# Attention with a gated feed-forward on one core: K turned as five windows of row pairs, x rows four to a partition, and a reordered opening of head 0 with norms on GpSimd

## The chip, the cores and the metric

The kernel runs on one core of one Trainium2 chip. The time is the device time of one execution in microseconds, and less is better. Executions are repeated in rounds, each round running the kernel in question and the kernel before on the same chip. The profile is one traced execution. Its engines are PE (TensorE, matmuls), PEld (its weight loads), DVE (VectorE), ACT (ScalarE), POOL (GpSimd) and SP (the engine that issues most DMAs). A program on one core has no second die to compare with.

## The reference, cut to what matters

```python
x:  (1, 2048, 640) bf16      k_cache, v_cache: (1, 32, 2048, 192) bf16
wq: (640, 32*192)            wo: (32*192, 640)       w1, w3: (640, 1536)   w2: (1536, 640)

xn = layernorm(x)                                   # over the 640 columns
q  = (xn @ wq) as 32 heads of 192
p  = softmax(q k^T * 192**-0.5)                     # 2048 x 2048 for each head
s  = concat_heads(p v) @ wo
g  = silu((silu(xn @ w1) * (xn @ w3)) @ w2)
out = x + s * g
```

## The kernel before

The 32 heads run one after the other as a stream of steps. A head has four blocks `qb` of 512 queries, a block has eight steps `p` of 256 keys. A step is: six score matmuls into a PSUM tile `st2`, one exponential of 128x1024 on ACT, and 16 value matmuls. Scores are written two steps ahead of values. At the start of block `qb` of head `h` stands the projection of q for head `h + 1`, block `qb`, so q is always one head ahead. Head 0 is special: nothing stands ahead of it, so x must be loaded, normed and transposed, K of head 0 must be transposed on PE, and q of head 0 itself must be projected block by block. This opening and head 0 are what the change rewrites.

K is needed transposed. It has 192 columns a key, and its matmuls go in pairs, one on rows 0 to 63 of PE and one on rows 64 to 127, which overlap (in the trace of the kernel before the two of a score pair start 18 ns apart and last 376 ns each). So the kernel before keeps three tiles a head: two from the transposing DMA, and KC, which two further DMAs fill with halves moved to the other 64 rows.

```python
def load_k(h):                                     # heads 1 to 31
    kh = A_k_cache[0, h]
    KA = kvp.tile([P, SK], BF16, ...); nc.sync.dma_start_transpose(out=KA[:], in_=kh[:, 0:P])
    KB = kvp.tile([P, SK], BF16, ...); nc.sync.dma_start_transpose(out=KB[:], in_=kh[:, DH - P:DH])

def copy_k(h):                                     # for h == 0 the same by ACT and DVE
    nc.gpsimd.dma_start(out=KC[64:P, :], in_=KA[0:64, HK:SK])
    nc.gpsimd.dma_start(out=KC[0:64, :], in_=KB[64:P, 0:HK])

def emit_scores(h, qb, p):                         # cut: each row is a pair, rows 0-63 and rows 64-127 of PE
    rounds = [(KA[0:64, lo], qAB[0][0:64, :], KA[64:P, hi], qAB[0][64:P, :]),
              (KB[0:64, lo], qC[0:64, 0, :],  KB[64:P, hi], qAB[1][64:P, :]),
              (KC[0:64, lo], qC[0:64, 1, :],  KC[64:P, lo], qC[64:P, 0, :])]

def ln_norm(g, i2):                                # cut; x group g of 512 rows is four tiles of 128
    for k in range(2):
        nc.vector.tensor_scalar(out=xn[:], in0=x_sb[:, 4 * g + i, :], scalar1=mv[:, i, 0:1], scalar2=rstd[:, i, 0:1],
                                op0=ALU.subtract, op1=ALU.mult)
        for c in range(DC):
            nc.tensor.transpose(out=pst[:, k, c, :], in_=xn[:, c * P:(c + 1) * P], identity=ident_bf[:])
    # cut: one copy to xnT, and after i2 == 1 two DMAs to xnS, the copy of xnT with its halves exchanged

# the opening, cut
transpose_k0(); ln_norm(0, 0); ln_norm(0, 1); project0(0, 1); project0(0, 0); copy_k(0)
for i in range(4): ln_stats(1, i)                  # DVE statistics; the power 1/sqrt runs on GpSimd
scores(0)
load_w(1); load_k(1); load_v(1)                    # W, K, V of head 1; load_w issues from GpSimd
scores(1)

for n, (h, qb, p) in enumerate(stream):            # cut
    if p == 0 and n > 0: project(h + 1, qb)
    scores(n + 2)
    if h == 0 and qb == 0 and p == 5: project(1, 0)          # the first use of W of head 1
    values(n)
    if h == 0 and qb + 1 < NQB:
        if p == 1 or p == 2: ln_norm(qb + 1, p - 1)
        if p == 3: project0(qb + 1, 1); project0(qb + 1, 0)  # q of head 0, next block
```

## Time and profile before

| | kernel before |
|---|---|
| time, median of 3 runs | 1957.51 us (1957.27 to 1957.65) |
| span of the profiled run | 1955.9 us |
| first exponential of head 0 (timeline) | 25.23 us |
| first exponential of head 1 (timeline) | 91.80 us |
| from head to head after that | 50.69 us |
| after the last exponential | 293.0 us |

The two lines that say what bounds it, from the page of the kernel before: the busy time of each engine with its share of the span, and the shares of the chain of work that ended last.

```profile
PE 1937.5 (99%) x27351; PEld 1390.2 (71%) x27351; DVE 654.1 (33%) x989; ACT 1184.2 (61%) x1277; POOL 319.2 (16%) x572
...
PE 98%; DVE 1%; DMA 1%; ACT 0%; issue 0%; DVEq 0%; ACTq 0%
```

PE is the bound nearly everywhere. What is left is in the table of waits of PE (kernel before; columns: who waited for what, total us, times, longest us):

```profile
engine line waited for: us in total, times, longest us
PE pk L255 <- DMA vt<-in_A_k_cache_dram: 4.6, 1, 4.6
PE warm L501 <- POOL ident_bf masks.py:199: 2.8, 1, 2.8
PE obank L449 <- DVE osum L459: 1.6, 2, 0.8
...
```

In the timeline of the kernel before (start, duration, engine, line, instruction), GpSimd issues the three loads of W of head 1 at 30.17 us, and the first projection that reads them starts at 38.47 us, after they have landed (35.28 us for the last):

```profile
30.17 0.89 POOL L225 DMA_DIRECT2D W<-in_A_wq_dram  x1
...
31.77 0.72 POOL L230 DMA_DIRECT2D W<-in_A_wq_dram  x1
...
38.47 0.37 PE L360 MATMUL ps<-xnT,W 64*128 64x512 bf16 x1
```

### The profile page before, as it was taken

The page shows a single profiled execution, that of the slowest core. Times are in us where ns is not written, and L with a number is a line of the kernel's source. Part 1 is how long each engine was busy: PE and PEld are TensorE (multiplying, and loading weights), DVE is VectorE, ACT ScalarE, POOL GpSimd, SP SyncE. Part 2 cuts the span into 40 slices and gives each one's busy share as a digit, 9 for nine tenths or more (in the row PEclk, how much of TensorE's full clock was granted, in tenths as well). Part 3 has the DMA queues.
Part 4 walks back from the last instruction along what each step waited for, and adds up shares of the span by engine and source line. Part 5 has one row for each costly group of instructions (what it writes and reads, how often), then busy time and mean ns, then how long its engine had stood idle before and what let it go on. Part 6 is the DMA issues. An engine that isn't in the chain of part 4 may idle for free.

```text
span 1955.9 us, 59887 instructions
## 1 busy us (share of the span) xinstructions
PE 1937.5 (99%) x27351; PEld 1390.2 (71%) x27351; DVE 654.1 (33%) x989; ACT 1184.2 (61%) x1277; POOL 319.2 (16%) x572
## 2 busy tenths in 40 slices
PE   7999999999999999999999999999999999999998
PEld 5677777777777777777777777777777777577776
DVE  5433333333333333333333333333333334521111
ACT  4667676767776767777777767776767777210000
POOL 3211111111111111111111111111111110000000
PEclk9999999999999999999999999999999999999999
DMA  7323232424343433363433243433323230937772
GB/s 178 80 65 93 59 96 67 94 64 100 68 100 68 100 68 97 67 160 68 100 68 100 65 99 68 97 71 77 88 57 93 58 85 2 247 69 140 155 152 60
DMA packets 362020, 177.95 MB, mean 91 GB/s; under 512 B 305712, under 2 KB 348976, under 8 KB 361760
## 3 DMA queue, kind: packets, MB, share of 16 engines
q1 hardware_dynamic: 334512, 116.21, 27.5%
q0 software_dynamic: 22736, 54.43, 11.3%
q8 instruction: 216, 3.54, 0.8%
q10 hardware_dynamic: 4512, 3.41, 0.6%
q14 instruction: 44, 0.36, 0.1%
HBM read 52.82 MB, written 27.79 MB: 41 GB/s over the span
## 4 chain that ended last, share of the span: by engine, by line
PE 98%; DVE 1%; DMA 1%; ACT 0%; issue 0%; DVEq 0%; ACTq 0%
PE obank L449 35%; PE st L420 31%; PE ps L360 14%; PE ps_s L106 11%; PE st L421 3%; PE ps_f L615 3%; PE ps_gu L589 1%; DMA vt<-in_A_k_cache_dram 1%; PE ps L341 0%; ACT pT L423 0%; DVE stats L295 0%; PE pst L311 0%; PE pk L255 0%; DMA qC<-qA 0%; ACT xnT L314 0%
## 5 line engine op out<-in xcount | busy, mean ns | idle before, releaser
L423 ACT ACTIVATE pT<-st 128x1024 bf16<-128x1024 f32 x1024 | 1046.3, 1022 | 257.5 <-PE st L421 242.0
L449 PEld LDWEIGHTS <-pT 64*128 64x128 bf16 x16384 | 743.2, 94 | 212.7 <-issue 2.5
L449 PE MATMUL obank<-vt,pT 64*128 64x193 bf16 x16384 | 866.2, 243 | 1.6 <-DVE osum L459 1.6
L420 PE MATMUL st<-qA,KA 64*128 64x512 bf16 x1024 | 385.4, 376 | 1.6 <-ACT pT L423 0.9
L420 PE MATMUL st<-qC,KB 64*128 64x512 bf16 x1024 | 385.3, 376 | 0.7 <-DMA qC<-qA 0.5
L420 PE MATMUL st<-qC,KC 64*128 64x512 bf16 x1024 | 385.3, 376 | 0.8 <-DVE KC L264 0.8
L421 PE MATMUL st<-qA,KA 64*128 64x512 bf16 x1024 | 385.6, 377 | 0.0
L421 PE MATMUL st<-qB,KB 64*128 64x512 bf16 x1024 | 385.5, 376 | 0.0
L421 PE MATMUL st<-qC,KC 64*128 64x512 bf16 x1024 | 385.5, 376 | 0.0
L458 DVE COPY osum<-obank 128x772 f32<-128x772 f32 x128 | 123.2, 962 | 784.0 <-PE obank L449 784.0
L360 PE MATMUL ps<-xnT,W 64*128 64x512 bf16 x1280 | 299.3, 376 | 0.0
L360 PE MATMUL ps<-xnS,W 64*128 64x512 bf16 x1280 | 294.0, 377 | 0.0
L330 POOL DMA_DIRECT2D qC<-qA x127 | 67.1, 528 | 1239.4 <-DVE rl_all L465 1235.9
L360 PEld LDWEIGHTS <-W 64*128 64x128 bf16 x2560 | 141.9, 94 | 104.8 <-issue 0.2
L366 ACT CAST qB<-ps 128x512 bf16<-128x512 f32 x128 | 74.9, 585 | 222.0 <-PE ps L360 222.0
L106 PE MATMUL ps_s<-wo_sb,oT 128*128 128x256 bf16 (+3 forms) x1536 | 208.8, 300 | 0.0
L106 PEld LDWEIGHTS <-oT 128*128 128x128 bf16 x1536 | 148.1, 98 | 60.7
L420 PEld LDWEIGHTS <-KC 64*128 64x128 bf16 x1024 | 96.4, 94 | 106.1 <-DVE KC L264 1.1
L459 DVE TENSOR_TENSOR osum<-osum,obank 128x772 f32<-128x772 f32 x128 | 122.7, 958 | 13.3
L466 DVE TENSOR_TENSOR ostage<-osum,rl_all 128x768 bf16<-128x768 f32 x128 | 122.6, 958 | 4.4
L401 DVE SCALAR_TENSOR_TENSOR hT<-pt,qB 64x512 bf16<-64x512 bf16 x64 | 43.8, 684 | 204.2 <-ACT pt L400 204.2
L420 PEld LDWEIGHTS <-KA 64*128 64x128 bf16 x1024 | 96.4, 94 | 15.8 <-issue 1.3
(77 smaller groups left out, 1151.1 us busy)
## 6 DMA issues: line engine op xcount, KB each, us to landing
vt<-in_A_v_cache_dram SPq DMA_DIRECT2D x32, 768.0 KB, 6.1
o_scr<-ostage SPq DMA_DIRECT2D x16, 1536.0 KB, 9.3
qC<-qA POOLq DMA_DIRECT2D x254, 64.0 KB, 1.9
qC<-qB POOLq DMA_DIRECT2D x127, 64.0 KB, 2.3
wo_sb<-in_A_wo_dram POOLq DMA_DIRECT2D x1, 7680.0 KB, 35.2
W<-in_A_wq_dram POOLq DMA_DIRECT2D x32, 160.0 KB, 3.3
KC<-KA POOLq DMA_DIRECT2D x31, 128.0 KB, 5.5
KC<-KB POOLq DMA_DIRECT2D x31, 128.0 KB, 5.5
```

Of the source, the lines that this page charges most:

```text
L106: nc.tensor.matmul(ps[:, 0:w], lhsT=oT[:, k, :], rhs=wo_sb[:, k, c0:c1], start=(k == 0), stop=(k == OC - 1))
L330: nc.gpsimd.dma_start(out=qC[0:64, half, :], in_=qAB[half][64:P, :])
L360: nc.tensor.matmul(ps[:, r * 512:(r + 1) * 512], lhsT=W[rows, j, :], rhs=xs[rows, j // 2, qs], start=(j == 0), stop=(j == 2 * DC - 1))
L366: b = nc.scalar.copy(out=qAB[1][:], in_=ps[:, 512:1024])
L420: nc.tensor.matmul(st2[:, 0:512], lhsT=k0, rhs=q0, start=r == 0, stop=r == 2)
L421: nc.tensor.matmul(st2[:, 512:1024], lhsT=k1, rhs=q1, start=r == 0, stop=r == 2)
L423: nc.scalar.activation(out=pT2[:], in_=st2[:], func=ACT.Exp, scale=att_scale)
L449: nc.tensor.matmul(obanks[r][:, j * 256:j * 256 + DH + 1], lhsT=pT2[r * 64:(r + 1) * 64, t * 512 + j * P:t * 512 + (j + 1) * P], rhs=vt[r ...
L458: nc.vector.tensor_copy(out=osum[:], in_=ov[0])
L459: nc.vector.tensor_tensor(out=osum[:], in0=osum[:], in1=ov[1], op=ALU.add)
L466: nc.vector.tensor_tensor(out=ostage[:, qb * 4:qb * 4 + 4, hg * DH:(hg + 1) * DH], in0=osum[:, :, 0:DH], in1=rl.unsqueeze(2).to_broadcast( ...
L615: nc.tensor.matmul(ps[:, b * 512:b * 512 + c1 - c0], lhsT=hT[:, fc, i * P:(i + 1) * P], rhs=w2_sb[:, fc, c0:c1], start=(fc == 0), stop=(fc ...
```

## The change

The intent: (1) two neighbouring keys are taken as one row of 384 values, and five windows of 128 of them, starting at 0, 128, 256, 64 and 192, are turned by DMA; every 64-row half that the scores need is then in place, and the KC copies fall away. V is loaded in the matching order, so the value matmuls of step `p` read tiles `2p` and `2p+1` of V instead of `p` and `8+p`. (2) x rows go four to a partition, so that a group's load reads 5120 bytes in one run. (3) The opening is reordered: x in two halves before K, norms of x on GpSimd, groups 2 and 3 of x turned by DMA instead of PE, the projection for head 1 at step 2 instead of 5, head 0's part of the feed-forward at step 3 instead of 6. The diff, cut to its core:

```diff
     def load_k(h):
-        kh = A_k_cache[0, h]
-        KA = ...; nc.sync.dma_start_transpose(out=KA[:], in_=kh[:, 0:P])
-        KB = ...; nc.sync.dma_start_transpose(out=KB[:], in_=kh[:, DH - P:DH])
+        pairs_of = A_k_cache[0, h].rearrange("(j two) d -> j (two d)", two=2)
+        KW = kvp.tile([P, 5, HK], BF16, tag="KW", name="KW")
+        nc.sync.dma_start_transpose(out=KW[:, 0:3, :], in_=pairs_of)
+        nc.sync.dma_start_transpose(out=KW[:, 3:5, :], in_=pairs_of[:, 64:64 + 2 * P])
-    def copy_k(h):  ...
 # emit_scores
-        rounds = [(KA[0:64, lo], qAB[0][0:64, :], KA[64:P, hi], qAB[0][64:P, :]), ...
+        rounds = [(KW[0:64, 0, ks], qA[0:64, :],    KW[64:P, 1, ks], qC[64:P, 0, :]),
+                  (KW[0:64, 3, ks], qC[0:64, 0, :], KW[64:P, 4, ks], qA[64:P, :]),
+                  (KW[0:64, 1, ks], qC[0:64, 1, :], KW[64:P, 2, ks], qB[64:P, :])]
 # load_x, and likewise x and out in the output stage
-                          in_=x2[g * 512:(g + 1) * 512, :].rearrange("(t p) d -> p t d", p=P))
+                          in_=x2[g * 512:(g + 1) * 512, :].rearrange("(p t) d -> p t d", t=4)[:, t0:t1, :])
+    def ln_norm(g, i, engine):        # one tile, on the engine that the caller names
+    def ln_turn_dma(g, i):            # groups 2 and 3
+        nc.sync.dma_start_transpose(out=xnT[:, :, q0:q0 + P], in_=xns.pop((g, i))[:])
 # the opening (cut)
+        ln_stats(0, 0); ln_stats(0, 1)
+        ln_norm(0, 0, nc.gpsimd); ln_norm(0, 1, nc.gpsimd)
+        ...
+        for i in range(4):
+            ln_stats(1, i)
+        for i in range(4):
+            ln_norm(1, i, nc.gpsimd)
+        load_w(1)                     # GpSimd too: behind the four norms
+        scores(0); load_k(1); load_v(1); scores(1)
 # the stream (cut)
-        if h == 0 and qb == 0 and p == 5:
+        if h == 0 and qb == 0 and p == 2:
             project(1, 0)
+        if h == 0 and qb + 1 < NQB and p == 4:
+            project0(qb + 1)
+        # after the statistics of group g = qb + 2 (steps 4 to 7 of block 0, 2 to 5 of block 1):
+                for t in range(4):
+                    ln_norm(g, t, nc.gpsimd)
+                    ln_turn_dma(g, t)
+                swap_halves(g)
```

## The prediction

> **What bounds it.** The page's busy shares give TensorE 99% (1937.5 of 1955.9 us); the chain of waits is 98% PE. In the timeline the first exponentials of heads 1 to 31 follow each other every 50.69 us without PE gaps. Head 0's starts at 25.23 us, head 1's at 91.8 us. The PE wait table lists 13.3 us of waiting, all before 80 us: 4.6 for K, 2.8 for the identity, 1.6 for obank. All that the change can win or lose is in these 91.8 us.
>
> **Steady state: no effect.** Matmuls per head stay the same. K comes as five transposed 128x1024 windows instead of two of 128x2048 plus two 128 KB copies: 1.25 times the transposed bytes, no KC copies. These land some 5 us after issue (DMA view), 50 us before use. Rows of x and out stay 1280 bytes or longer.
>
> **Opening, gain about 5.5 us.** x arrives as two 320 KB halves ahead of K; estimate 4.4 us for the first (640 KB landed at 5.7). Stats 2.1, power 0.73, two GpSimd norms: no line exists for one; from the 128x128 select at 0.30 us I estimate 1.05 us for 640 columns, against 0.44 on DVE. The Trainium skill, "GPSIMD Engine Reference", section 4.1, calls one-input GpSimd work roughly line-rate; no run here shows it yet. K's transposes fit beside this; without KC copies and the ACT/DVE ping-pong over q, the first exponential should start near 19.6 us.
>
> **Head 0, loss about 13 us.** In instruction order GpSimd issues W of head 1 only after the four norms of x group 1, whose stats DVE runs only after the q copies. Stats end near 22.5, power 23, norms 27.5, three issues (0.73-0.85 each) 30, landing (3.5 us after issue before) about 33 us. The projection for head 1 has moved from step 5 to step 2, which PE reaches near 23.5 us: **a PE wait of about 9 us**. Such a gap also halves the granted clock: before, it fell to 0.5 after 3.2 us of idleness and stayed so to 5.4 us after work resumed (clock records). "TensorE: Matmul & The Clock Gate", section "The HAM clock gate", describes that; I allow 2 us.
>
> Further waits: 2.5 us before the second block's projection (its transposes come just before it, their DVE copy behind the tanh); 3.5 to 4 us for x group 2 (stats end after osum, four serial norms, DMA transposes[...], against four steps plus one projection); 1 us at each of three qC moves.
>
> Saved: PE transposes for groups 2 and 3, 3 us, and their copies.
>
> **Sum.** Laying instructions out with these durations by engine order reproduces 91.7 us for the kernel before, and gives 97 us after, 99 with the slow clock: about 5 to 7 us longer. I shade down: a reordered opening was presumably meant to fit its loads.
>
> **Predicted: 1962 us, 1948 to 1971.** Faster by over 2%: 0.01; within 2%: 0.98; slower by over 2%: 0.01.
>
> **Right or wrong if:** first exponential near 19-21 us; a PE wait of 6-11 us on W (or L387) around 23-33 us with a clock dip; first exponential of head 1 at 93-102 us; head period still 50.69 us; GpSimd norm 0.8-1.4 us.
>
> **What would make it wrong:** norms far faster or slower than 1 us (seven lie in series ahead of W); W landing early; DMA transposes from SBUF taking 5 us or more; GpSimd and DVE blocking each other.

## More of the kernel before

The windows view cuts the span where head 0 and head 1 begin (kernel before; length, then busy us of PE, PEld, DVE, ACT, POOL with their instructions, the granted TensorE clock as a share of full speed, DMA share, GB/s):

```profile
0.00:25.20 25.20, 15.49 (x140) 12.75 (x142) 9.80 (x28) 8.35 (x7) 4.96 (x11) 0.86 0.88 216
25.20:91.80 66.60, 62.96 (x850) 43.37 (x848) 34.98 (x79) 41.31 (x46) 20.99 (x35) 1.00 0.41 91
91.80:1663.00 1571.20, 1571.20 (x24314) 1136.22 (x24310) 540.76 (x753) 1113.40 (x1181) 282.37 (x509) 1.00 0.35 80
```

In head 0 PE is idle for 3.6 of 66.6 us, at full clock; from head 1 to the last exponential it is never idle.

## The result

The changed kernel takes 1992.07 us (median of 4 runs, 1989.96 to 1992.8) against 1957.49 us (1957.27 to 1957.65) for the kernel before. The ratio is 1.0175, 95% interval 1.0157 to 1.0193: slower by 1.75%, within 2%. Ratios here and below are the mean time of one kernel's fast runs over that of the other's of the same rounds, so not quite the ratio of the quoted medians.

Where the 34.4 us of span (1990.3 less 1955.9) went, read from the starts of the first exponentials in the two timelines:

| stretch | before | after | difference |
|---|---|---|---|
| to the first exponential of head 0 | 25.23 | 22.12 | -3.1 |
| from there to the first exponential of head 1 | 66.57 | 102.12 | +35.6 |
| from there to the end of the last exponential | 1571.1 | 1573.1 | +2.0 (50.75 for 50.69 us a head) |
| after it | 293.0 | 293.0 | 0.0 |

The page of the changed kernel, the same two lines:

```profile
PE 1943.8 (98%) x27310; PEld 1508.1 (76%) x27317; DVE 647.4 (33%) x976; ACT 1180.0 (59%) x1274; POOL 325.1 (16%) x525
...
PE 95%; POOL 2%; issue 1%; DMA 1%; DVE 1%; ACT 0%; POOLq 0%; DVEq 0%
```

The windows of the changed kernel, cut at its own head starts (same columns as before):

```profile
0.00:22.10 22.10, 14.44 (x150) 12.51 (x151) 9.86 (x31) 6.01 (x6) 12.32 (x14) 0.85 0.80 235
22.10:124.20 102.10, 68.55 (x803) 41.83 (x805) 29.02 (x64) 39.83 (x45) 50.34 (x45) 0.82 0.35 74
124.20:1697.00 1572.80, 1572.80 (x24308) 1255.36 (x24304) 539.65 (x751) 1112.73 (x1180) 251.61 (x449) 1.00 0.35 80
```

In head 0 PE is idle for 33.5 us (102.1 less 68.55) instead of 3.6. It is also busy for 5.6 us longer with fewer instructions: the granted clock averages 0.82 there, where it was 1.00. The table of waits of PE (changed kernel) names the waits:

```profile
PE ps L374 <- DMA xnT<-xn: 14.2, 2, 10.6
PE ps L387 <- DMA W<-in_A_wq_dram: 14.1, 2, 13.7
PE pst L322 <- POOL xn L314: 4.9, 2, 3.1
...
PE ps L374 <- DVE xnT L324: 2.1, 1, 2.1
...
```

Two rows of the table make 28 us. The first names a DMA, but what it waited for began on GpSimd. The timeline of the changed kernel around the wait on W:

```profile
25.68 0.69 POOL L307 TENSOR_TENSOR rstd<-ve,mhalf 128x2 f32<-128x2 f32 x1 [1.51 <-DVE ve L306]
26.36 9.95 POOL L314 TENSOR_SCALAR xn<-x_all,mv,rstd 128x640 bf16<-128x640 bf16 x4
36.25 0.82 POOL L231 DMA_DIRECT2D W<-in_A_wq_dram  x1
...
37.78 0.72 POOL L236 DMA_DIRECT2D W<-in_A_wq_dram  x1
39.77 0.61 PE L387 MATMUL ps<-xnT,W 64*128 64x512 bf16 x1 [13.74 <-DMA W<-in_A_wq_dram]
```

Four norms take 9.95 us on GpSimd, 2.49 us each, and the issue of W stands behind them in GpSimd's own order. PE had stopped at 26.03 us. The wait on the transposing DMA, in the same timeline some 40 us later, has the same cause:

```profile
65.81 10.73 POOL L314 TENSOR_SCALAR xn<-x_all,mv,rstd 128x640 bf16<-128x640 bf16 x4
69.12 8.66 SPq L328 DMA_TRANSPOSE xnT<-xn  x4
...
80.43 0.58 PE L374 MATMUL ps<-xnT,W 128*128 128x512 bf16 x1 [10.61 <-DMA xnT<-xn]
```

The four DMA transposes are issued at 69.12, 71.61, 74.09 and 76.58 us, each as its norm ends, 2.5 us apart; three of them land 2.6 us after their issue and the last 3.6. In the packed trace, clock records show the full clock halved around the three long waits (26.0 to 39.8, 69.8 to 80.4 and 98.4 to 102.0 us) and after the one of 2.1 us (50.0 to 52.1): from 29.4 to 46.5, 53.3 to 56.8, 73.8 to 84.1 and 101.1 to 108.0 us, 37.5 us in all, much of it after the work had resumed.

### The profile page after: what moved, and what is told of

The parts are those of the page before. It is cut to its first block, busy times and chain, and to the rows that moved or that the text cites. A ratio compares the mean times of both kernels' runs of the same rounds, so it can differ in the third digit from the quotient of the medians.

```text
span 1990.3 us, 59747 instructions
## 1 busy us (share of the span) xinstructions
PE 1943.8 (98%) x27310; PEld 1508.1 (76%) x27317; DVE 647.4 (33%) x976; ACT 1180.0 (59%) x1274; POOL 325.1 (16%) x525
## 3 DMA queue, kind: packets, MB, share of 16 engines
q1 hardware_dynamic: 370880, 126.44, 29.4%
## 4 chain that ended last, share of the span: by engine, by line
PE 95%; POOL 2%; issue 1%; DMA 1%; DVE 1%; ACT 0%; POOLq 0%; DVEq 0%
PE obank L474 35%; PE st L446 25%; PE ps L387 14%; PE ps_s L111 10%; PE st L445 6%; PE ps_f L674 3%; POOL xn L314 1%; PE ps_gu L648 1%; PE ps L374 1%; DMA xnT<-xn 0%; POOL rstd L307 0%; DVE stats L302 0%; DMA W<-in_A_wq_dram 0%; DMA qC<-qA 0%; PE pk L269 0%
## 5 line engine op out<-in xcount | busy, mean ns | idle before, releaser
L474 PE MATMUL obank<-vt,pT 64*128 64x193 bf16 x16384 | 1041.9, 243 | 0.0
L474 PEld LDWEIGHTS <-pT 64*128 64x128 bf16 x16384 | 923.9, 94 | 104.1 <-issue 1.4
L445 PE MATMUL st<-qC,KW 64*128 64x512 bf16 x2048 | 607.8, 377 | 0.0
L445 PE MATMUL st<-qA,KW 64*128 64x512 bf16 x1024 | 385.8, 377 | 1.6 <-ACT pT L448 1.6
L446 PE MATMUL st<-qC,KW 64*128 64x512 bf16 x1024 | 385.8, 377 | 1.0 <-DMA qC<-qA 1.0
L446 PE MATMUL st<-qB,KW 64*128 64x512 bf16 x1024 | 385.8, 377 | 0.0
L446 PE MATMUL st<-qA,KW 64*128 64x512 bf16 x1024 | 385.8, 377 | 0.0
L446 PEld LDWEIGHTS <-KW 64*128 64x128 bf16 x3072 | 278.6, 94 | 126.6 <-issue 3.3
L387 PE MATMUL ps<-xnT,W 64*128 64x512 bf16 x1280 | 302.2, 378 | 13.7 <-DMA W<-in_A_wq_dram 13.7
L445 PEld LDWEIGHTS <-KW 64*128 64x128 bf16 x3072 | 278.5, 94 | 8.4 <-issue 4.9
L387 PE MATMUL ps<-xnS,W 64*128 64x512 bf16 x1280 | 257.4, 378 | 0.4 <-DMA W<-in_A_wq_dram 0.4
L387 PEld LDWEIGHTS <-W 64*128 64x128 bf16 x2560 | 165.3, 94 | 117.1 <-DMA W<-in_A_wq_dram 14.0
L111 PE MATMUL ps_s<-wo_sb,oT 128*128 128x384 bf16 (+3 forms) x1535 | 208.8, 299 | 0.1
L392 DVE CAST qA<-ps 128x512 bf16<-128x512 f32 x131 | 90.5, 691 | 67.6 <-PE ps L387 45.8
## 6 DMA issues: line engine op xcount, KB each, us to landing
o_scr<-ostage SPq DMA_DIRECT2D x16, 1536.0 KB, 10.2
```

The lines of the kernel that those rows point to most:

```text
L111: nc.tensor.matmul(ps[:, 0:w], lhsT=oT[:, k, :], rhs=wo_sb[:, k, c0:c1], start=(k == 0), stop=(k == OC - 1))
L387: nc.tensor.matmul(ps[:, r * 512:(r + 1) * 512], lhsT=W[rows, j, :], rhs=xs[rows, j // 2, qs], start=(j == 0), stop=(j == 2 * DC - 1))
L392: a = nc.vector.tensor_copy(out=qAB[0][:], in_=ps[:, 0:512])
L445: nc.tensor.matmul(st2[:, 0:512], lhsT=ka, rhs=qa, start=r == 0, stop=r == 2)
L446: nc.tensor.matmul(st2[:, 512:1024], lhsT=kb, rhs=qb2, start=r == 0, stop=r == 2)
L474: nc.tensor.matmul(obanks[r][:, j * 256:j * 256 + DH + 1], lhsT=pT2[r * 64:(r + 1) * 64, t * 512 + j * P:t * 512 + (j + 1) * P], rhs=vt[r ...
```

## The experiments

The theory after the result, **A**: the norm on GpSimd is far longer than estimated and stands in series ahead of the load of W and of the DMA transposes; the order of issue (W behind the norms) is the other half of it. The rivals: **B**, the DMA transposes of groups 2 and 3 are slow in themselves; **C**, the waits are as predicted, and the halved clock is the larger part; and for the 0.06 us a head, that the K windows, the pairing of operands or the x rows make it. (The new order of V, a fourth, was not on the list; a trace speaks for it below, under e11.)

| run | what it is | time (median, us) | ratio to before, 95% interval | head 1's first exponential | us a head |
|---|---|---|---|---|---|
| before | | 1957.5 | | 91.8 | 50.69 |
| changed | | 1992.07 | 1.0175 (1.0157 to 1.0193) | 124.2 | 50.75 |
| e1 | changed, norms on VectorE | 1970.04 | 1.0067 (1.0050 to 1.0084) | 102.7 | 50.75 |
| e2 | changed, W issued before the norms | 1979.18 | 1.0114 (1.0097 to 1.0130) | 111.5 | 50.75 |
| e3 | changed, PE kept busy in the waits | 1986.48 | 1.0148 (1.0131 to 1.0165) | 119.4 | 50.75 |
| e4 | before, K windows and V order alone | 1956.86 | 0.9997 (0.9980 to 1.0014) | 89.0 | 50.75 |
| e5 | e1 and e2 together | 1962.96 | 1.0026 (1.0011 to 1.0042) | 95.4 | 50.75 |
| e6 | before, with probes of the norm | 1957.14 (one run) | | 91.1 | 50.69 |
| e7 | e5, rearranged | 1952.69 | 0.9974 (0.9960 to 0.9988) | 84.9 | 50.75 |
| e8 | e4, the other half of PE first | 1957.86 (one run) | | 90.2 | 50.75 |
| e9 | e7, rearranged again | 1953.75 | 0.9983 (0.9969 to 0.9996) | 84.8 | 50.75 |
| e10 | before, x rows alone | 1957.08 | 0.9998 (0.9982 to 1.0013) | 90.9 | 50.69 |
| e11 | before, pairing of the changed kernel | 1958.26 (one run) | | 92.5 | 50.69 |
| e12 | e9, K load further back in the program | 1954.04 | 0.9979 (0.9966 to 0.9993) | 85.1 | 50.75 |

### e1: the norms on VectorE

```diff
-        ln_norm(0, 0, nc.gpsimd)          # and the same for every norm of groups 0 to 3
+        ln_norm(0, 0, nc.vector)
```

> The changed kernel with all its norms on VectorE (0.44 us each in the trace) instead of GpSimd (2.49 us each); orders, DMA transposes and the K windows stay. Theory A (the slow GpSimd norms, in series ahead of the load of W for head 1 and of the DMA transposes, are the cause): the wait on W shrinks from 13.7 to about 5 us, the two waits on the DMA transposes from 14.2 to under 3 us, the first exponential of head 1 comes at 91 to 95 us instead of 124.2, the time is 1958 to 1964 us. Rival B (the DMA transposes of x groups 2 and 3 are slow in themselves): their waits stay above 8 us and the time stays above 1975 us.

Measured: 1970.04 us, 22.0 us less than the changed kernel, but 12.5 us more than the kernel before, and outside the expected 1958 to 1964. The waits of PE in e1:

```profile
PE ps L387 <- DMA W<-in_A_wq_dram: 9.5, 2, 7.0
PE st L446 <- DMA qC<-qA: 3.2, 3, 1.7
PE pk L525 <- POOL ident_bf masks.py:199: 2.8, 1, 2.8
PE st L445 <- DVE qA L392: 2.2, 1, 2.2
PE ps L374 <- DVE xnT L324: 2.1, 1, 2.1
PE pk L269 <- DMA kn<-in_A_k_cache_dram: 1.9, 1, 1.9
PE st L445 <- ACT pT L448: 1.1, 1, 1.1
PE pst L322 <- DVE xn L314: 0.4, 1, 0.4
```

That is the whole table: the DMA transposes are no longer in it, with the same transposes of the same tiles still issued (they landed 2.6 to 4.6 us after their issue). **Rival B falls.** The wait on W shrank less than expected. GpSimd issues W at 23.69 us, 12.6 us sooner, but the transfers take 6.5 to 7.9 us to land instead of 2.9 to 3.5: they now run at the same time as the two transposing loads of K of head 1 (issued 16.35 and 23.66, landed 26.6 and 33.2). So theory A was right in kind and too simple: the issue of W is late even with fast norms, since it still follows the statistics of group 1.

### e2: W issued before the norms

```diff
         swap_halves(0)
+        load_w(1)
         ...
         for i in range(4):
             ln_norm(1, i, nc.gpsimd)
-        load_w(1)
```

> The changed kernel with nothing but the load of W for head 1 issued before the four norms of x group 1; all norms stay on GpSimd. Theory A: the wait of 13.7 us on W is gone and with it the clock dip at 29 to 46 us; the waits on the DMA transposes stay near 14 us; first exponential of head 1 at 102 to 108 us, time 1970 to 1976 us. If W was not a true bottleneck (rival: the norms of group 1 themselves hold the transposes, and the wait only moves), the time stays above 1985 us.

Measured: 1979.18 us, first exponential of head 1 at 111.5 us, both about 3 us beyond the expected ranges, but 12.9 us less than the changed kernel. The wait on W is gone from the table of waits; the waits on the DMA transposes stand at 14.3 us, as expected, and 5 shorter waits of PE on the norms of groups 0 and 1 make 8.5 us in all, against 4.9:

```profile
PE ps L374 <- DMA xnT<-xn: 14.3, 2, 10.6
PE pst L322 <- POOL xn L314: 8.5, 5, 2.3
...
```

That is the part of the rival that is true: some 3.6 us of the wait moved from W to the transposes on PE that wait for a norm.

### e3: PE kept busy while it waits

```diff
+    def fill(ps, k):
+        for i in range(k):
+            nc.tensor.matmul(ps[:, 0:P], lhsT=ident_bf[:], rhs=ident_bf[:], start=True, stop=True)
 # in the tile that the projection then overwrites: 200 ahead of project(1, 0); 20, 150, 40 ahead of project0(1), (2), (3)
```

> The changed kernel with throw-away 128-column matmuls put before the three kinds of stalled projections, into the PSUM tile that the projection then overwrites, so that TensorE is busy while it waits. Waits unchanged. Theory C (about a third of the loss is the halved clock after the waits): granted clock near 1.0 from 25 to 124 us, first exponential of head 1 at 112 to 117 us, time 1980 to 1985 us. If the clock cost what was predicted (2 us), the time is 1989 to 1991 us. The fillers themselves should fit into the waits.

Measured: 1986.48 us, 5.6 us less than the changed kernel. The window of head 0 in e3:

```profile
21.60:119.40 97.80, 87.92 (x1214) 62.47 (x1214) 29.03 (x64) 39.81 (x45) 50.35 (x45) 0.95 0.36 78
```

The clock rose from 0.82 to 0.95, not to 1.0: the fillers ran out 1.3 to 2.3 us before the long waits ended, and 10.2 us of halved clock are left in the records of head 0 (38.9 to 45.7 and 79.8 to 83.2 us), against 37.5 in the changed kernel. Not all of the 5.6 us can be put down to the fillers. Of the 4.9 us between the two profiled runs, 4.3 lie in head 0 (97.8 for 102.1); 0.5 lie in the opening, which holds no filler: there the changed kernel's trace has a clock record of 6.8 us and e3's has none, by chance, as the code is the same. So the halved clock costs **at least some 4 us** in head 0, not the 2 that the prediction allowed, and running warm did not give back the 7 to 12 that were expected of this run. Rival C as the main cause falls: of the 34.6 us lost, 29 stay with the clock at 0.95.

### e4: the K windows and the V order alone

```diff
 # the kernel before, with load_k, emit_scores, the V order and head 0's five windows of the changed kernel; no copy_k;
 # old x layout, old order of the opening, norms on VectorE
+        for w0, w1 in ((0, 2), (2, 4), (4, 5)):
+            ...  # 16, 16 and 8 transposes of kn on PE, one copy by ACT each
```

> The kernel before with the five K windows, the matching V order and no KC copies, but the old x layout and the old opening. If the K windows are neutral in the steady state, as predicted, a head takes 50.69 us and the time is 1955 to 1960 us (40 instead of 32 transposes in the opening, but no KC copies on the chain). If they are what makes a head 0.06 us longer in the changed kernel (50.75 us), the time is about 1.9 us longer than that, 1957 to 1962 us, and the head period reads 50.75 us.

Measured: 1956.86 us, ratio 0.9997: neutral in time, but not for the reason predicted. The head takes 50.75 us here too, which costs 31 x 0.06 = 1.9 us, and the opening pays for it: the first exponential of head 0 comes at 21.45 instead of 25.23 us, as no KC copies stand between the projection and the third pair of scores and the clock was not halved in this run's opening. The second of these is luck: e8 has the same opening, but for the order within pairs of matmuls, and a clock record of 6.8 us in it, and starts at 23.31. Head 0 itself is 1 us longer (67.57). So the 2.0 us of the table above belong to this part of the change.

### e5: both edits

The diffs of e1 and e2 together.

> Both edits together: all norms on VectorE, and the load of W for head 1 issued before the norms of x group 1. With norms on VectorE alone, 9.5 us of waiting on W[...] were left, because the issue still came behind the stats of group 1 and its transfer ran into the K load of head 1. Theory A (norm time and issue order together are the whole loss): the wait on W is gone, first exponential of head 1 at 88 to 92 us, time 1955 to 1960 us. If something else in the reordered opening costs (rival), the time stays above 1963 us.

Measured: 1962.96 us (1959.88 to 1965.53, a wide spread), 29.1 us less than the changed kernel, and 3 us over the expected range. The wait on W is gone. What is left against the kernel before is 5.4 us: the opening is 6.8 us shorter (first exponential at 18.45), the heads 2 us longer, and head 0 10.3 us longer (76.9 us), by waits of 2.8 us on the exchange of halves of x, 2.6 on the DMA transposes, 2.2 on a DVE cast behind the norms, 2.1 on the DVE copy of group 1 and 1.9 on q moves (the DMAs that bring halves of q to the other 64 rows), and three clock records of 3.4 us. The rival (something else in the reordering costs) holds for these few us. I read them as the order of the steps itself; e7 makes that likely, but no run changes that alone.

### e6: the norm by itself

```diff
+        # steps 5 of heads 3 to 5; x0 = x_sb[:, 0, :], s0 and s1 columns of mhalf; nothing reads prb
+        nc.gpsimd.tensor_scalar(out=prb[:, 0:w], in0=x0[:, 0:w], scalar1=s0, scalar2=s1, op0=ALU.subtract, op1=ALU.mult)
+        # and: one operation; constants -0.5; tensor_copy; tensor_tensor; the same on nc.vector
```

> The kernel before with eleven extra elementwise instructions in heads 3 to 5, where GpSimd is idle, into tiles that nothing reads: the norm's form on GpSimd at 640, 320 and 160 columns, one operation alone, constants in place of per-partition scalars, a plain copy, a sum of two inputs; and the norm's form on VectorE. If the 2.49 us are a rate (3.9 ns a column), 320 columns take about 1.3 us and 160 about 0.7; if they are a fixed cost of the instruction, all widths take over 2 us. If the per-partition scalars or the second operation make it slow, the forms without them take about 0.6 to 1.1 us; if not, all take over 2 us. VectorE about 0.4 us. No effect on the time.

The timeline of e6, with the probes' lines alone (L286 the norm's form, L289 one operation with a per-partition scalar, L291 two operations with constants, L298 the norm's form on VectorE):

```profile
200.24 2.51 POOL L286 TENSOR_SCALAR prb<-x_all,mhalf 128x640 bf16<-128x640 bf16 x1
211.90 1.44 POOL L286 TENSOR_SCALAR prb<-x_all,mhalf 128x320 bf16<-128x320 bf16 x1
224.59 0.90 POOL L286 TENSOR_SCALAR prb<-x_all,mhalf 128x160 bf16<-128x160 bf16 x1
...
251.01 1.90 POOL L289 TENSOR_SCALAR prb<-x_all,mhalf 128x640 bf16<-128x640 bf16 x1
262.58 2.39 POOL L291 TENSOR_SCALAR prb<-x_all 128x640 bf16<-128x640 bf16 x1
275.22 0.73 POOL L293 COPY prb<-x_all 128x640 bf16<-128x640 bf16 x1
290.03 1.42 POOL L295 TENSOR_TENSOR prb<-x_all 128x640 bf16<-128x640 bf16 x1
300.25 0.43 DVE L298 TENSOR_SCALAR prd<-x_all,mhalf 128x640 bf16<-128x640 bf16 x1
```

It is a rate: from 160 to 640 columns the time grows by 1.61 us, 3.35 ns a column, over a fixed part of about 0.37 us. Leaving out one operation saves 0.6 us, constants save 0.1; neither makes it cheap. A plain copy of the same columns takes 0.73 us and a sum of two tiles 1.42. (VectorE was at work for 1.25 us of the sum and 0.68 of the one-operation form, so these two may be lengthened.) The norm is 5.8 times as long on GpSimd as on VectorE (2.51 to 0.43), and with VectorE idle, so no quarrel of the two engines is needed: in the changed kernel the four norms of group 1 took 2.50 us each while VectorE stood idle. One of its norms (at 65.81 us) took 3.29, while VectorE was at work; such a quarrel could explain this 0.8 us, but not the rest.

### e7: a version built from the findings

```diff
 # e5, and:
+        if qb == 0 and p == 2: ln_turn(1, 0, ...); ln_turn(1, 1, ...); swap_halves(1)     # one step earlier, both by DVE
-        (project(1, 0) at p == 2, project0 at p == 4, swiglu at p == 3)
+        (project(1, 0) and project0 at p == 3, swiglu at p == 6)
+        at = {(0, 3): (2, 0), (0, 5): (2, 1), (1, 1): (3, 0), (1, 3): (3, 1)}             # norms and DMA turns two tiles at a time
+        if qb == 0 and p == 6: load_k(1); load_v(1)                                       # instead of in the opening
```

> A version built from the findings: norms on VectorE, W of head 1 early, x groups 2 and 3 normed and sent to the DMA transpose two tiles at a time from the first block on, the K and V loads of head 1 after them, group 1's transposes one step ahead of the projections that read it, and the projections of head 0 one step earlier (step 3). First exponential of head 0 near 19.5 us, of head 1 at 79 to 84 us, no wait over 2 us after 25 us, no clock dip after 25 us, time 1946 to 1953 us: faster than the kernel before by about 0.4%.

Measured: 1952.69 us, ratio 0.9974 with an interval of 0.9960 to 0.9988: 0.26% faster than the kernel before, and faster than the changed kernel by 39 us. First exponentials at 19.54 and 84.94 us, the second 0.9 us later than expected. The windows of e7 show the full clock over head 0 and PE idle for 6.6 of 65.4 us:

```profile
0.00:19.50 19.50, 14.84 (x150) 13.00 (x151) 11.13 (x33) 6.00 (x6) 7.09 (x14) 0.91 0.94 236
19.50:84.90 65.40, 58.77 (x801) 39.79 (x803) 33.30 (x76) 37.97 (x43) 17.53 (x30) 1.00 0.62 124
```

Its longest waits on a DMA in head 0 are 1.6 us on a q move (to 54.1 us), 1.1 on a DMA transpose (to 64.1) and 0.9 on a q move (to 71.8). The first falls in the time when the K load of head 1 is on its way (issued 44.95 and 51.13, landed 54.6 and 56.1 us); the second is for a tile that landed in 4.5 us, in a group whose first transpose was issued while the loads of K and V were on their way (V landed by 59.2); the third comes when both have long landed.

### e8: the other half of PE first

```diff
 # e4 with the two matmuls of every score pair exchanged, and in values:
-                for r in range(2):
+                for r in (1, 0):
```

> The kernel with the K windows alone (e4), with the matmuls of rows 64 to 127 written before those of rows 0 to 63 in the score and the value products. In e4 a head takes 50.75 us against 50.69 before, and the trace shows that the two halves of a pair start in the other order there. If that order makes the 0.06 us, the head period returns to 50.69 us; if it is the operands or the loads, it stays at 50.75 us.

Measured: 50.75 us a head, as in e4 (one run, 1957.86 us). The order in which the two halves of a pair are written does not make the 0.06 us. The expectation took the two nearest starts in e4 for a pair, but they belong to different pairs: rows 0 to 63 of a pair still start first there, about 197 ns ahead instead of 18. That distance is not the cause either: it is 197 ns in e11, at 50.69 us a head, and 19 in e5, at 50.75.

### e9: e7 with two of its collisions moved

```diff
-        if qb == 0 and p == 6: load_k(1); load_v(1)
+        if qb == 1 and p == 6: load_k(1); load_v(1)
+        # statistics of a pair of tiles one step ahead of their norms: (0,2)/(0,3), (0,4)/(0,5), (1,1)/(1,2), (1,4)/(1,5)
```

> The better version again, with the two things its trace showed: the K and V loads of head 1 go behind the last x group (they ran into the q moves and the DMA transposes, three waits of 1.6, 1.1 and 0.9 us), and the stats of groups 2 and 3 stand one step ahead of their norms, so that VectorE does not stand waiting for the powers of GpSimd in front of osum. First exponential of head 1 at 80 to 83 us instead of 84.9, time 1947 to 1951 us; if those waits are only replaced by others, 1952 to 1953 us.

Measured: 1953.75 us, ratio 0.9983: a miss, no better than e7. The three waits are replaced by one of 3.3 us on a q move with a clock record of 3.4 us behind it, near 67 us, where the K load now is (issued 57.74 us).

### e10: the x rows alone

```diff
-                          in_=x2[g * 512:(g + 1) * 512, :].rearrange("(t p) d -> p t d", p=P))
+                          in_=x2[g * 512:(g + 1) * 512, :].rearrange("(p t) d -> p t d", t=4))
 # and the matching rows of x and out in the output stage; everything else as before
```

> The kernel before with nothing but the x rows taken four to a partition (one 5120-byte run a partition in the x loads, row pitch of four in the last stage's loads and stores). Every part of the theory says that this is neutral: 1955 to 1958 us, at most 1 us gained because x arrives sooner. If the strided rows of the last stage cost anything, the time rises by over 2 us with the head period unchanged.

Measured: 1957.08 us, ratio 0.9998, 50.69 us a head. Neutral, as expected.

### e11: the pairing of the changed kernel, with the old K tiles

```diff
-        rounds = [(KA[0:64, lo], qAB[0][0:64, :], KA[64:P, hi], qAB[0][64:P, :]),
-                  (KB[0:64, lo], qC[0:64, 0, :], KB[64:P, hi], qAB[1][64:P, :]),
-                  (KC[0:64, lo], qC[0:64, 1, :], KC[64:P, lo], qC[64:P, 0, :])]
+        rounds = [(KA[0:64, lo], qAB[0][0:64, :], KC[64:P, lo], qC[64:P, 0, :]),
+                  (KB[0:64, lo], qC[0:64, 0, :], KA[64:P, hi], qAB[0][64:P, :]),
+                  (KC[0:64, lo], qC[0:64, 1, :], KB[64:P, hi], qAB[1][64:P, :])]
```

> The kernel before with the three pairs of score matmuls made up as in the changed kernel (qA with the lower copy of qC, qC with qA, qC with qB), the K tiles and all loads as before. If it is the pairing of the operands that makes a head 0.06 us longer, the head period reads 50.75 us; if it is the K windows' loads or layout or the V order, 50.69 us.

Measured: 50.69 us a head (one run, 1958.26 us). The pairing does not make the 0.06 us either.

The traces kept here say where the 0.06 us are, if one takes the starts of the matmuls of one row half and averages them over some 660 steps. From one score matmul to the next they are 215.8 ns apart in every kernel. From the third score matmul to the first of the next step, with eight value matmuls between, it is 882.5 ns in the kernel before, e10 and e11, and 884.5 in the changed kernel, e4, e5, e7 and e8. These 2.0 ns in each of 32 steps are the 0.06 us a head. They arise where the value matmuls go over to the second 128 keys: the fifth starts 87.5 ns after the fourth instead of 83.3, and the next ones make up for about half of it. Of what a value matmul reads, the change moves V alone there (from tile `2p` to `2p+1`, instead of from `p` to `8+p`). So the score matmuls on the K windows are not it, and loads, which come once a head, are unlikely. No run changes the order of V alone, so the cause stays open.

### e12: the K load further back

```diff
-        if qb == 1 and p == 6: load_k(1); load_v(1)
+        if qb == 2 and p == 5: load_k(1); load_v(1)
```

> The second better version (e9) with the K and V loads of head 1 moved once more, from step 6 of the second block to step 5 of the third, behind the last q moves of head 0. In e9 these loads ran into those moves (qC from qB landed 6.2 us after its issue) and made one wait of 3.3 us with a clock dip. If that is all, the first exponential of head 1 comes at 79 to 82 us and the time is 1947 to 1951 us; if the loads then come too late for head 1 itself, a wait on KW near 80 us shows and the time stays at 1952 to 1954 us.

Measured: 1954.04 us, ratio 0.9979: a miss. The loads did not move. The timeline of e12 shows the issue on SP:

```profile
54.91 0.62 SPq L333 DMA_DIRECT2D xnS<-xnT  x1
55.58 6.18 SPq L252 DMA_TRANSPOSE KW<-in_A_k_cache_dram  x1
...
63.00 0.52 POOL L347 DMA_DIRECT2D qC<-qA  x1
```

The K load is issued at 55.58 us, right behind the last exchange of halves, although its place in the program comes later (the exponential of step 5 of the third block starts at 62.32 us). It depends on nothing (its buffer is fresh), so SP issues it as soon as it has issued what stands before it. The q move issued at 63.00 us then landed at 69.85, and PE waited 4.2 us for it. Later in the program is not later in time for a DMA without a dependency; e9's gain was lost to the same collision: there the second part of K, issued at 63.27 us, and a q move issued at 63.93 both landed near 70.3. e7, e9 and e12 differ by less than the spread of their runs (e12's five runs go from 1950.95 to 1954.14 us).

## Why the prediction was wrong

Predicted were 1962 us (1948 to 1971); measured 1992.07. The sign, the place and the mechanism were right; two terms of the sum were too small.

- **The mis-sized term: "from the 128x128 select at 0.30 us I estimate 1.05 us for 640 columns".** This is the step that failed: the cost of a norm on GpSimd. It takes 2.49 us in the changed kernel and 2.51 alone (e6). The estimate scaled one instruction of another kind, and leaned on the Trainium skill, "GPSIMD Engine Reference", section 4.1, for one-input work being roughly line-rate. e6 gives 0.73 us for a copy, which does not contradict that sentence; the two-operation form on bf16 takes 3.4 times as long for the same columns, so the sentence does not carry over to it. The measurement decides. The prediction named this as its first way to be wrong ("norms far faster or slower than 1 us"), but its range did not allow for a factor of 2.4.
- **"A PE wait of about 9 us" on W** was 13.7 + 0.4 us. Its chain was told correctly, step by step: statistics end at 25.6 (said: 22.5), the last power at 26.4 (23), norms at 36.3 (27.5), issues at 38.5 (30), PE resumes at 39.8 (33). Nearly all of the slip is the norms: the four here took 5.4 us more than forecast, and the later end of the statistics goes back to the three in the opening (with norms on VectorE, in e1, they end at 22.9). PE resumed 1.3 us after the last issue, not 3, as it could start on the first of the three parts. e2 shows that taking W out of this order is worth 12.9 us.
- **"3.5 to 4 us for x group 2"** was 10.6 us, and group 3, given none, 3.6 us. The DMA transposes themselves were not the slip (2.6 us from issue to landing, in one of four 3.6); the four norms ahead of them were. With the norms on VectorE these waits are gone (e1).
- **"I allow 2 us" for the halved clock** was the second term too small. The longer waits make more and longer clock records, 37.5 us in head 0. Running warm gave 4.3 us back in head 0 with records of 10.2 us left (e3), so this is a lower bound. "TensorE: Matmul & The Clock Gate", section "The HAM clock gate", gives about 3.4 us as the window of the activity monitor; every record of halved clock in these traces, but for the last of each, which stands at the end of the execution, is a multiple of that (3.41, 6.83, 10.24, 17.07 us), which agrees.
- **"Opening, gain about 5.5 us"** was 3.1 us, for the same norms: the transposes of group 0 waited 4.9 us for them. With norms on VectorE it is 5.9 (e1).
- **"2.5 us before the second block's projection"** was 2.1 us. "1 us at each of three qC moves" was 1.0 us in all.
- **"Head period still 50.69 us"** was wrong by 0.06 us a head, 2.0 us in all; it belongs to the K and V part (e4) and is neither the pairing (e11) nor the order of the halves (e8) nor the x rows (e10). The traces place it in the value matmuls, where V is read in its new order; the mechanism is open.
- The hand layout, an estimate from trace durations, gave 91.7 us for the kernel before (91.8 measured) and 97 for the changed one, where 124.2 was measured. A part of the difference is the halved clock, for which the forecast added 2 us: PE's busy time in head 0 grew by 5.6 us although 40 transposes (four sets of ten at about 0.7 us) were gone, from which I estimate some 8 us.

So the sum is: 22.0 us for the norms' engine (e1), 12.9 for the place of W (e2), 29.1 for both together (e5; the two overlap), with the clock's share inside these; the remaining 5.4 us are head 0's other waits, which I put down to the order of the steps, and the 0.06 us a head, less the shorter opening. That the change could gain at all is shown by e7, which keeps its K windows, x rows and DMA transposes, and runs 0.26% ahead of the kernel before.

## What to carry to other kernels

Before moving an instruction to another engine, find a duration of that very form there, operation, type and width, or measure it alone in an idle stretch of the kernel; an estimate from a different instruction needs a range as wide as the doubt. Ask what stands behind the moved instruction in the new engine's own order: here three DMA issues that had nothing to do with the norms stood behind four of them, and moving them ahead alone was worth 12.9 us (e2); the long waits of PE were paid for again in clock. A DMA that depends on nothing goes out as soon as its queue comes to it, whatever its line in the program (e12: at 55.58 us, right behind the issue before it).

## What the Trainium skill lacked or had wrong

- "GPSIMD Engine Reference", section 4.1: "1-input is roughly line-rate" is not contradicted by a copy (0.73 us for 128x640 bf16) but does not hold for the arithmetic that a norm needs, one input with scalars: 1.90 us with one operation, 2.51 us with two, 2.39 with constants for the scalars, against 0.43 us on VectorE. The section gives no figure for this form; the runs give 3.35 ns a column over about 0.37 us.
- "GPSIMD Engine Reference": it does not say outright that a DMA issued from GpSimd waits behind elementwise work in the same engine's order; here three issues of W waited 9.95 us behind four norms.
- "TensorE: Matmul & The Clock Gate", section "The HAM clock gate": its table puts the half clock after at least one idle window of about 3.4 us. Here waits shorter than that were followed by it: one of 2.1 us in the changed kernel (50.0 to 52.1 us, record from 53.3 to 56.8; PE was busy for 1.24 of the 3.41 us before the record) and one of 2.8 us in e5 (22.6 to 25.3, record from 26.4 to 29.9).
- "DMA: Bandwidth & Descriptors" has no time from issue to landing for a small transpose from SBUF to SBUF: a 128x640 one landed 2.6 us after its issue when alone, up to 6.2 us while other transfers ran (e7).
- No page was found that gives a cause for value matmuls of which the fifth starts 87.5 instead of 83.3 ns after the fourth when V is read from the neighbouring tile (2.0 ns a step after all, 50.75 for 50.69 us a head, with the same count of matmuls); it is left open here.
